# Packed attention and a gated MLP on one core: a W' piece and half a score product side by side, from unit 40 on in written order

## The chip, the cores and the metric

The kernel runs on one core of one Trainium2 chip. The metric is the device time of one execution in microseconds (us), the median of several runs. Engines are named as the profile names them: PE is TensorE (PEld its weight loads), DVE is VectorE, ACT is ScalarE, POOL is GpSimd, SP is SyncE. PSUM, where TensorE writes, has eight banks.

## The reference

```python
batch, n_heads, seq, head_dim = (8, 8, 576, 64)      # q, k, v: (8, 8, 576, 64); p: (8, 8, 32, 64)
n_tokens, d_model, d_ff = (4608, 512, 2048)

def sm_attn(qq, kk, vv):
    s = scale * np.matmul(qq, kk.transpose(0, 1, 3, 2))   # scale = 1/8
    a = np.exp(s - np.max(s, axis=-1, keepdims=True))
    return np.matmul(a / (np.sum(a, axis=-1, keepdims=True) + 1e-09), vv)
p_packed = sm_attn(p, k, v)                # 32 packed rows for each head
out = sm_attn(q, p_packed, p_packed)
x = out.transpose(0, 2, 1, 3).reshape(4608, 512)
h = x @ w_in
sp = np.maximum(h, 0.0) + np.log1p(np.exp(-np.abs(h)))
g = h * erf(sp)
return g @ w_out
```

## The kernel before, in words

Attention never forms x. For each batch b it computes the packed rows (pt, 32 for each head), multiplies them with w_in once (W', the tiles wp: 32 x 8 rows by 2048 columns, in four pieces of 512, `w_prime`), and the second softmax (a2) is then the moving operand: h = a2 x W'. Precise products are made of three reduced ones: a tile is split into a high part and a rest (wph and wpl, a2h and a2l, gh and gl, wohl).

The MLP runs in units. A unit is one batch, one half of its tokens (288) and 256 of the 2048 columns: 12 matmuls of h (`h_half`, two halves of six, each into one of two PSUM banks, ps_h), copies out by ScalarE (`h_copy`, tile hs), the gate, and 24 matmuls of o (`o_part`, four parts d of six, accumulated over the eight units of a half in four banks, ps_o). From unit 32 on, the gate is made of four ScalarE passes and three VectorE passes: tanh, square and tanh again (t, t, u), two products and sums on VectorE, a third tanh (t), the product with hs; then the split into gh and gl. Units 0 to 31 are batches 0 and 1; batch b from 2 on has the units 16b to 16b + 15, 128 in all. The o of a unit is issued three units later (LAG). After eight units `put` copies the four banks out (ob) and stores them.

The attention of a batch runs beside the units of the batch ahead of it. `attention(b)` is a generator: each `yield` ends a step that can be placed by itself. Its parts are the loads of k, v and q (SP's queue, through a ring of six buffers), the first scores in two halves (s1, from p and k), the first softmax, the turned scores (t1 and p on TensorE), pooling with v, the packed rows pt, the second scores in two halves (s2, from pt and q), and `second_softmax`. The halves, the turned chunks and the W' pieces all use one PSUM tile of two banks, ps_m. The matmuls of W' and of the scores are small tiles, 64 rows by 32 columns of TensorE's array; h and o use all 128 x 128.

`plan_attention` spreads the steps of batch b over the first seven units of batch b-1, and the four W' pieces of batch b stand at the units 9, 11, 13 and 15 of batch b-1. Inside this plan, a scheduler that simulates a timeline sets the order on each engine; only the beginning (up to unit 19) is a written list. `keep_order` ties instructions of one engine to the order in which they were recorded.

Of the kernel before, what the change touches and what calls it, by code (L numbers as in the profile page):

```python
# [8 lines left out]
F32 = mybir.dt.float32  # L9
# [5 lines left out]
AF = mybir.ActivationFunctionType  # L15
# [33 lines left out]
def tile_pack_attention_moe(ctx: ExitStack, tc: tile.TileContext, qT, kT, v, pT, w_in, w_out, outT):  # L49
# [157 lines left out]

    def attention(b):

        fine, roomy = b < NB0, b == 0  # L210
        at_o = {0: {"s1_0": 0, "s1_1": 2, "p": 0, "s2_0": 2, "s2_1": 0}, 1: {"s1_0": 0, "s1_1": 2}}.get(b, {})

        def chunk(name, tag="kvq"):
# [3 lines left out]
                return opool.tile([P, S], F32, name=f"{name}_{b}", tag="wo")[:]  # L217
            return tpool.tile([P, S], F32, name=f"{name}_{b}", tag=tag)[:]

        def bank(name):  # L220

            if name in at_o:
                d = at_o[name]
                return [ps_o.tile([P, 512], F32, name=f"{name}_{b}_{x}", tag=f"ps_o{d + x}")[:] for x in range(2)], None
            ps = ps_m.tile([P, 2, 512], F32, name=f"{name}_{b}", tag="ps_m")
            return [ps[:, 0, :], ps[:, 1, :]], ps
# [19 lines left out]
        values = [chunk(f"v{j}", v_at[j]) for j in range(NCH)]  # L246
        for j in range(NCH):
            n, t0 = (CH, j * CH) if j < NT else (REM, NT * CH + (j - NT) * REM)
            nc.sync.dma_start(values[j][0:n, 0:2 * NC * 64], v[b, t0:t0 + n, :])
        yield  # L250
        q_at = ("t0", "t0", "t0", "t1") if roomy else ("wo",) * NC if b == 1 else ("kvq",) * NC
        q = [chunk(f"q{c}", q_at[c]) for c in range(NC)]
        for c in range(NC):
            nc.sync.dma_start(q[c], qT[b, :, c, :])
        yield
        a1 = apool.tile([P, 2, S], F32, name=f"a1_{b}", tag="big", bufs=3)
        scores = []
        for c2 in range(2):
            banks = bank(f"s1_{c2}")
            for c in range(NC):  # L260
                for r in range(2):
                    nc.tensor.matmul(banks[0][r][NK * c:NK * c + NK, 0:HT], p[64 * r:64 * r + 64, c, :],  # L262
                                     k[c][64 * r:64 * r + 64, c2 * HT:(c2 + 1) * HT], start=True, stop=True)
            if roomy:
                scores.append(banks[0])
            else:
                if fine:
                    yield
                copy_out(a1[:, :, c2 * HT:(c2 + 1) * HT], banks, HT)
            yield  # L270
        m = apool.tile([P, 2], F32, name=f"m{b}", tag="m")
        sm = apool.tile([P, 2], F32, name=f"sm{b}", tag="sm")
        a1t = apool.tile([P, 2, NCH, P], F32, name=f"a1t{b}", tag="big", bufs=3)
# [32 lines left out]
        if roomy:  # L306
            sums = apool.tile([P, 2, 2], F32, name=f"sums{b}", tag="parts")
            for r in range(2):
                for c2 in range(2):
                    nc.scalar.activation(a1[:, r, c2 * HT:(c2 + 1) * HT], scores[c2][r][:, 0:HT], AF.Exp,  # L310
                                         bias=m[:, r:r + 1], scale=SCALE, accum_out=sums[:, r, c2:c2 + 1])
                yield
            turned = [ps_h.tile([P, 512], F32, name=f"t1_{b}", tag="ps_h")[:], bank("t1")[0][1]]
            po, pr = bank("p")[0]
            for r, (copy, rest) in enumerate(((nc.vector.tensor_copy, po), (nc.scalar.copy, pr))):
                turn_chunks(r, turned[r])
                turn_rest(r, rest)
                yield
                copy(a1t[0:CH, r, 0:NT].rearrange("p j k -> p (j k)"), turned[r][0:CH, 0:NT * P])
                copy(a1t[0:REM, r, NT:NCH].rearrange("p j k -> p (j k)"), rest[0:REM, 0:NR * P])  # L320
                yield
            for r in range(2):
                pool(r, po)
                yield
            nc.vector.tensor_reduce(sm[:], sums[:], axis=AX.X, op=ALU.add)
        else:
            for r in range(2):
                nc.scalar.activation(a1[:, r, :], a1[:, r, :], AF.Exp, bias=m[:, r:r + 1], scale=SCALE,
                                     accum_out=sm[:, r:r + 1])
                if fine or r:  # L330
                    yield
            (turned, turned1), banks = bank("t1")
            turn_chunks(0, turned)
            turn_chunks(1, turned1)
            if fine:
                yield
            nc.scalar.copy(a1t[0:CH, :, 0:NT].rearrange("p r j k -> p r (j k)"), banks[0:CH, :, 0:NT * P])
            yield
            (po, pr), _ = bank("p")
            for r in range(2):  # L340
                turn_rest(r, pr[:, r * NR * P:(r + 1) * NR * P])
            if fine:
                yield
            nc.scalar.copy(a1t[0:REM, :, NT:NCH].rearrange("p r j k -> p r (j k)"),
                           pr[0:REM, 0:2 * NR * P].rearrange("p (r k) -> p r k", r=2))
            if fine:
                yield
            for r in range(2):
                pool(r, po)
            if fine:  # L350
                yield
        nc.vector.tensor_scalar(sm[:], sm[:], 1e-9, None, op0=ALU.add)
        nc.vector.reciprocal(sm[:], sm[:])
        if fine:
# [11 lines left out]
        yield  # L366
        ta = apool.tile([P, 2, S], F32, name=f"ta{b}", tag="big", bufs=3)
        for c2 in range(2):
            banks = bank(f"s2_{c2}")
            for c in range(NC):  # L370
                for r in range(2):
                    nc.tensor.matmul(banks[0][r][NK * c:NK * c + NK, 0:HT], ptt[64 * r:64 * r + 64, NK * c:NK * c + NK],  # L372
                                     q[c][64 * r:64 * r + 64, c2 * HT:(c2 + 1) * HT], start=True, stop=True)
# [13 lines left out]
        if roomy:  # L387
# [4 lines left out]
        every = second_softmax(b, ta, tb, mx, hi, lo, 0, S, None, nc.vector.tensor_copy if fine else nc.scalar.copy)  # L392
        for k, _ in enumerate(every):
            if fine or k in (2, 8):
                yield
# [115 lines left out]
    def split_for(n):  # L511
        while unsplit and unsplit[0] in (n, n + 1):
            split_high(unsplit[0])
            split_low(unsplit.pop(0))

    def h_block(n):
        for k in range(2):
            h_half(n, k)
            h_copy(n, k)
        if n < GROUPED:  # L520
# [5 lines left out]
                unsplit.extend(group)  # L526
                group.clear()
            return
        b, c, i = units[n][:3]
        hs = rows.pop(n)  # L530
        t = tpool.tile([P, 2, HT], F32, name=f"t{b}_{c}_{i}", tag="t0")
        u = tpool.tile([P, 2, HT], F32, name=f"u{b}_{c}_{i}", tag="t1")
        nc.scalar.activation(t[:], hs[:], AF.Tanh, bias=bias[:, 0:1], scale=2.0 * T_SCALE)  # L533
        nc.scalar.activation(t[:], t[:], AF.Square, bias=bias[:, 1:2], scale=Q_SCALE)  # L534
        nc.scalar.activation(u[:], t[:], AF.Tanh, bias=bias[:, 2:3], scale=U_SCALE)  # L535
        nc.vector.scalar_tensor_tensor(t[:], t[:], 0.5 * A2, hs[:], op0=ALU.mult, op1=ALU.add)  # L536
        nc.vector.scalar_tensor_tensor(t[:], u[:], 0.5 * A1, t[:], op0=ALU.mult, op1=ALU.add)  # L537
        nc.scalar.activation(t[:], t[:], AF.Tanh, bias=bias[:, 3:4], scale=2.0 * A_SCALE)  # L538
        nc.vector.scalar_tensor_tensor(hs[:], t[:], 1.0, hs[:], op0=ALU.add, op1=ALU.mult)  # L539
        gs[n] = (hs,)  # L540
        while unsplit:
            split_high(unsplit[0])
            split_low(unsplit.pop(0))
        split_high(n)
        split_low(n)

    def o_block(n):

# [20 lines left out]

    def at(n):
        return plan.setdefault(n, [])

    plan, whole_w, ready = {}, {}, {}
    attended = {NB0: ATTENDED}

    def plan_attention(b):
        free = last_of[b - 2] + 1
        start, end = free, free + 6  # L580
        if b == NB0:
# [12 lines left out]
    for k, (b, j) in enumerate(uses):  # L594
        if b < NB0:
            whole_w[b] = 0
            continue
        if b not in ready:
            plan_attention(b)
        n = max(ready[b], last_use[uses[k - NFB]])  # L600
        at(n).append(("wp", b, j))
        whole_w[b] = n

    gens = {}
# [19 lines left out]
    def keep_order(start, end):  # L624

        last = {}
        for k, ins in enumerate(traced[start:]):
# [42 lines left out]
        elif n in gs and len(gs[n]) == 1 and n >= WHOLE:  # L670
            unsplit.append(n)
    behind = BEHIND
    for n in range(BEGUN, len(units) + LAG):
        if n < len(units):
            grouping[0] = n < GROUPED
            items = plan.pop(n, [])
# [45 lines left out]
```

## Time and profile before

| what | value |
|---|---|
| median of 3 runs | 730.31 us (729.38 to 730.31) |
| the profiled execution's own time | 729.3 us |
| its span | 727.5 us |
| granted TensorE clock | 0.999 |
| PE, PEld, DVE, ACT busy | 713.7, 653.0, 542.8, 576.1 us |
| one batch (382.91 to 470.07) | 87.16 us |
| large matmuls: mean length of a record | 0.30 us (o, 128x128 by 288) |
| W' pieces: records, busy | 528, 37.4 us |
| first and second scores: records, busy | 256 and 256, 12.2 and 11.2 us |

The length of a matmul's record is a latency: the next one starts well before it ends, so what a matmul costs is read from one start to the next. Each small matmul of W' and the scores is two records, so a W' piece or a half (8 matmuls) shows as 16. In rows of the timeline the columns are start, length, engine, line, operation, tiles out and in, shapes, count, and in brackets the idle time ahead with what ended it.

### The profile page before, as it was taken

What the parts mean: (1) busy time and instruction counts of PE and PEld (TensorE: products, weight loads), DVE (VectorE), ACT (ScalarE), POOL (GpSimd) and SP (SyncE); (2) the same over time, 40 slices, a digit from 0 to 9 for tenths busy, and PEclk for the clock granted to TensorE, in tenths of its full rate; (3) what the DMA queues carried; (4) which work ended last, traced back from release to release, by engine and by line L of the source; (5) the groups of instructions that cost most, each with busy time, mean ns of one, the idle gap of its engine ahead of it and who ended that gap; (6) DMA issues with size and microseconds to landing.
All of it is one profiled execution on the core that took longest, in us unless ns stands there. A gap on an engine that the chain in (4) does not pass through costs nothing.

```text
span 727.5 us, 15459 instructions
## 1 busy us (share of the span) xinstructions
PE 713.7 (98%) x6416; PEld 653.0 (90%) x6416; DVE 542.8 (75%) x835; ACT 576.1 (79%) x971; POOL 36.2 (5%) x56
## 2 busy tenths in 40 slices
PE   6799999999999999999999999999999999999998
PEld 4587989999889898998899998999899998899997
DVE  4989986446666897769967698767977689776674
ACT  3799988967678697887888778786887969787883
POOL 2011111121111000000000000000000000000000
PEclk9999999999999999999999999999999999999999
DMA  9965542253134210221103220023100211000001
GB/s 319 398 203 177 174 169 84 86 122 78 21 62 107 96 33 1 86 87 62 35 1 90 83 71 26 1 86 116 62 2 1 86 50 34 1 26 9 9 26 34
DMA packets 30855, 58.42 MB, mean 80 GB/s; under 512 B 3648, under 2 KB 12864, under 8 KB 30784
## 3 DMA queue, kind: packets, MB, share of 16 engines
q1 hardware_dynamic: 27424, 52.11, 21.4%
q0 software_dynamic: 3072, 4.72, 3.7%
q8 instruction: 50, 0.82, 0.5%
q10 hardware_dynamic: 288, 0.59, 0.2%
q14 instruction: 21, 0.17, 0.1%
HBM read 45.61 MB, written 11.80 MB: 79 GB/s over the span
## 4 chain that ended last, share of the span: by engine, by line
PE 96%; DVE 2%; POOL 1%; ACT 0%; issue 0%; ACTq 0%; POOLq 0%
PE o L492 57%; PE h L441 28%; PE wp L403 5%; PE p L289 1%; PE s L262 1%; PE s L372 1%; PE t L277 1%; POOL w_in_sb L95 0%; PE p L282 0%; PE idle L640 0%; DVE w_in_sb L116 0%; DVE wpl L420 0%; DVE ta L182 0%; DVE ta L186 0%; DVE mx L184 0%; DVE m L302 0%
## 5 line engine op out<-in xcount | busy, mean ns | idle before, releaser
L492 PE MATMUL o<-gh,wohl 128*128 128x288 f32 x1984 | 421.4, 297 | 0.0
L492 PEld LDWEIGHTS o<-gh,wohl 128*128 128x128 f32 x1984 | 325.3, 188 | 14.2 <-issue 7.3
L492 PE MATMUL o<-gl,wohl 128*128 128x288 f32 x992 | 293.0, 296 | 0.0
L492 PEld LDWEIGHTS o<-gl,wohl 128*128 128x128 f32 x992 | 186.7, 188 | 0.1
L441 PE MATMUL h<-a2h,wph 128*128 128x288 f32 x512 | 154.1, 301 | 0.3 <-DVE wph L416 0.3
L441 PE MATMUL h<-a2h,wpl 128*128 128x288 f32 x512 | 151.4, 296 | 0.7 <-DVE wpl L420 0.7
L441 PE MATMUL h<-a2l,wph 128*128 128x288 f32 x512 | 150.9, 295 | 0.0
L451 ACT ACTIVATE hs<-h 128x288 f32<-128x288 f32 x192 | 77.9, 411 | 62.5 <-PE h L441 59.4
L539 DVE SCALAR_TENSOR_TENSOR hs<-t,hs 128x576 f32<-128x576 f32 x96 | 72.6, 757 | 66.5 <-ACT t L538 66.5
L441 PEld LDWEIGHTS h<-a2h,wph 128*128 128x128 f32 x512 | 96.1, 188 | 23.4 <-ACT u L535 8.4
L476 DVE TENSOR_TENSOR gl<-hs,gh 128x576 fp32r<-128x576 f32 x124 | 93.5, 754 | 8.9 <-ACT gh L469 6.9
L538 ACT ACTIVATE t<-t,bias 128x576 f32<-128x576 f32 x96 | 74.1, 772 | 31.5 <-DVE t L537 31.4
L441 PEld LDWEIGHTS h<-a2h,wpl 128*128 128x128 f32 x512 | 96.1, 188 | 2.0 <-DVE wpl L420 1.2
L441 PEld LDWEIGHTS h<-a2l,wph 128*128 128x128 f32 x512 | 96.1, 188 | 0.8 <-issue 0.8
L536 DVE SCALAR_TENSOR_TENSOR t<-t,hs 128x576 f32<-128x576 f32 x96 | 72.1, 751 | 20.0 <-ACT u L535 20.0
L469 DVE CAST gh<-hs 128x576 fp32r<-128x576 f32 x119 | 54.3, 457 | 31.6 <-PE o L492 29.5
L533 ACT ACTIVATE t<-hs,bias 128x576 f32<-128x576 f32 x96 | 74.6, 777 | 2.4
L534 ACT ACTIVATE t<-t,bias 128x576 f32<-128x576 f32 x96 | 74.4, 775 | 2.2
L535 ACT ACTIVATE u<-t,bias 128x576 f32<-128x576 f32 x96 | 74.4, 775 | 1.5
L537 DVE SCALAR_TENSOR_TENSOR t<-u,t 128x576 f32<-128x576 f32 x96 | 72.2, 752 | 1.2
L420 DVE TENSOR_TENSOR wpl<-wp,wph 128x1024 fp32r<-128x1024 f32 (+1 forms) x33 | 38.9, 1179 | 8.3 <-ACT wph L416 8.0
L403 PE MATMUL wp<-w_in_sb,pt 64*32 64x512 f32 (+1 forms) x528 | 37.4, 588 | 3.7 <-DVE w_in_sb L116 3.7
(85 smaller groups left out, 591.5 us busy)
## 6 DMA issues: line engine op xcount, KB each, us to landing
q<-qT SPq DMA_DIRECT2D x32, 288.0 KB, 4.5
k<-kT SPq DMA_DIRECT2D x30, 288.0 KB, 4.2
wos<-w_out SPq DMA_DIRECT2D x16, 512.0 KB, 5.7
outT<-ob SPq DMA_DIRECT2D x48, 144.0 KB, 2.1
v<-v SPq DMA_DIRECT2D x24, 256.0 KB, 4.1
wi<-w_in SPq DMA_DIRECT2D x12, 512.0 KB, 6.9
outT<-ob POOLq DMA_DIRECT2D x32, 144.0 KB, 3.3
v<-v SPq DMA_DIRECT2D x16, 192.0 KB, 3.8
```

The lines of the kernel that those rows point to most:

```text
L403: nc.tensor.matmul(ps[NK * c:NK * c + NK, r, 0:n], pt[b][64 * r:64 * r + 64, NK * c:NK * c + NK], w_in_sb[64 * r:64 * r + 64, c, f0:f0 + n ...
L441: nc.tensor.matmul(ps[:, 0:HT], w[:, r, fo:fo + P], a[:, r, c * HT:(c + 1) * HT], start=(m == 0), stop=(m == 5))
L451: nc.scalar.mul(dst, src, 0.5)
L476: nc.vector.tensor_tensor(glo[:], hs[:], ghi[:], op=ALU.subtract)
L492: nc.tensor.matmul(acc[b, c, d][:, 0:HT], w[f][:, d * P:(d + 1) * P], gg[:, k, :], start=(first and k == 0 and m == 0), stop=(last and k = ...
L533: nc.scalar.activation(t[:], hs[:], AF.Tanh, bias=bias[:, 0:1], scale=2.0 * T_SCALE)
L534: nc.scalar.activation(t[:], t[:], AF.Square, bias=bias[:, 1:2], scale=Q_SCALE)
L535: nc.scalar.activation(u[:], t[:], AF.Tanh, bias=bias[:, 2:3], scale=U_SCALE)
L536: nc.vector.scalar_tensor_tensor(t[:], t[:], 0.5 * A2, hs[:], op0=ALU.mult, op1=ALU.add)
L537: nc.vector.scalar_tensor_tensor(t[:], u[:], 0.5 * A1, t[:], op0=ALU.mult, op1=ALU.add)
L538: nc.scalar.activation(t[:], t[:], AF.Tanh, bias=bias[:, 3:4], scale=2.0 * A_SCALE)
L539: nc.vector.scalar_tensor_tensor(hs[:], t[:], 1.0, hs[:], op0=ALU.add, op1=ALU.mult)
```

## The change

From unit 40 on the program is recorded step by step (`step`) and the order of TensorE, VectorE and ScalarE is kept as recorded; SP's queue is still the scheduler's. Within a step stand the unit's h, the third tanh and the product of the unit before, then the four parts of o, with the gate passes of this unit behind part 0 and the split of the unit before behind them.

For the batches 4 to 7 ("joined") the steps of attention get places of their own, relative to the first unit F of the batch ahead (`ATTEND`: unit, and where in it). The four W' pieces of the batches 3 to 6 are put at F-6, F-4, F+2 and F+4 of their own batch (`JOINS`), and so behind part 0 of o, directly ahead of a score half of the next batch: s1 at F-6 and F-4, s2 at F+2 and F+4. The last batch's pieces stand alone at F-7, F-5, F-3 and F-1 (`ALONES`). W' keeps ps_m; the halves now use the two banks of h (ps_h), since ps_m holds W'. First-score halves are then copied out in two copies of 288. v is loaded behind the first scores and q behind pooling. Where W' is written into wph (ScalarE) and wpl (VectorE) is the end of the step.

TensorE before, with buffer numbers kept (wp4_0 is piece 0 of batch 4, s1_0_5 the first half of batch 5's first scores, h3_1_1_0 a half of h of batch 3, o3_0_0_3 part 3 of an o). The W' piece stands between o and h of units 56 and 57:

```order
L492 MATMUL o3_0_0_3_3980<-gl3_0_5_4084,wohl11_1325 128x288
L492 MATMUL o3_0_0_3_3980<-gh3_0_5_4082,wohl11_1325 128x288
L403 MATMUL wp4_0_4297<-w_in_sb_81,pt4_4018 32x512 x8
L441 MATMUL h3_1_1_0_4311<-a2h3_2997,wph3_0_3205 128x288
L441 MATMUL h3_1_1_0_4311<-a2l3_2998,wph3_0_3205 128x288
```

The half stands alone too, eight units later, behind h of unit 65:

```order
L441 MATMUL h4_0_1_1_4826<-a2l4_4099,wph4_0_4306 128x288
L441 MATMUL h4_0_1_1_4826<-a2h4_4098,wpl4_0_4307 128x288
L262 MATMUL s1_0_5_4856<-k0_5_4775,p5_4773 32x288 x2
L262 MATMUL s1_0_5_4856<-k1_5_4776,p5_4773 32x288 x2
L262 MATMUL s1_0_5_4856<-k2_5_4777,p5_4773 32x288 x2
L262 MATMUL s1_0_5_4856<-k3_5_4778,p5_4773 32x288 x2
L492 MATMUL o3_1_0_0_4473<-gh3_1_6_4648,wohl12_1327 128x288
```

TensorE with the change, in unit 58 (F-6 of batch 4, whose first unit is 64), behind part 0 of o:

```order
L513 MATMUL o3_0_0_0_3949<-gh3_0_7_4279,wohl15_1571 128x288
L424 MATMUL wp4_0_4387<-w_in_sb_81,pt4_3807 32x512 x8
L279 MATMUL s1_0_5_0_4397<-k0_5_4069,p5_4067 32x288
L279 MATMUL s1_0_5_1_4398<-k0_5_4069,p5_4067 32x288
L279 MATMUL s1_0_5_0_4397<-k1_5_4070,p5_4067 32x288
L279 MATMUL s1_0_5_1_4398<-k1_5_4070,p5_4067 32x288
L279 MATMUL s1_0_5_0_4397<-k2_5_4071,p5_4067 32x288
L279 MATMUL s1_0_5_1_4398<-k2_5_4071,p5_4067 32x288
L279 MATMUL s1_0_5_0_4397<-k3_5_4072,p5_4067 32x288
L279 MATMUL s1_0_5_1_4398<-k3_5_4072,p5_4067 32x288
L513 MATMUL o3_0_0_1_3967<-gh3_0_7_4279,wohl14_1449 128x288
```

The piece has moved from the end of unit 56 into unit 58, the half from unit 65 into the same place; the half has a tile for each bank (s1_0_5_0, s1_0_5_1). The ScalarE list of unit 58 before (h copies of unit 58 first, those of unit 59 last but one):

```order
L451 ACTIVATE hs3_1_2_4364<-h3_1_2_0_4365 128x288
L451 ACTIVATE hs3_1_2_4364<-h3_1_2_1_4373 128x288
L533 ACTIVATE t3_1_2_4381<-hs3_1_2_4364,bias_80 128x576
L501 COPY ob3_0_7_0_4418<-o3_0_0_0_3959 128x288
L203 CAST a2h4_4098<-tb4_4097 128x1152
L534 ACTIVATE t3_1_2_4381<-t3_1_2_4381,bias_80 128x576
L501 COPY ob3_0_7_1_4421<-o3_0_0_1_3966 128x288
L501 COPY ob3_0_7_2_4424<-o3_0_0_2_3973 128x288
L538 ACTIVATE t3_1_1_4327<-t3_1_1_4327,bias_80 128x576
L501 COPY ob3_0_7_3_4427<-o3_0_0_3_3980 128x288
L535 ACTIVATE u3_1_2_4382<-t3_1_2_4381,bias_80 128x576
L451 ACTIVATE hs3_1_3_4443<-h3_1_3_0_4444 128x288
```

The same list with the change, from behind the h copies of unit 58 to its end:

```order
L550 ACTIVATE t3_1_1_4329<-t3_1_1_4329,bias_80 128x576
L522 COPY ob3_0_7_0_4384<-o3_0_0_0_3949 128x288
L243 COPY a1_5_4396<-s1_0_5_0_4397 128x288
L243 COPY a1_5_4396<-s1_0_5_1_4398 128x288
L543 ACTIVATE t3_1_2_4409<-hs3_1_2_4359,bias_80 128x576
L545 ACTIVATE t3_1_2_4409<-t3_1_2_4409,bias_80 128x576
L546 ACTIVATE u3_1_2_4410<-t3_1_2_4409,bias_80 128x576
L522 COPY ob3_0_7_1_4426<-o3_0_0_1_3967 128x288
L522 COPY ob3_0_7_2_4435<-o3_0_0_2_3974 128x288
L522 COPY ob3_0_7_3_4444<-o3_0_0_3_3981 128x288
L208 CAST a2h4_4132<-tb4_4131 128x1152
L437 CAST wph4_0_4449<-wp4_0_4387 128x1024
```

The third tanh of the unit before (t3_1_1) now stands ahead of the first tanh of this one, the two copies of the half stand between, and the a2h and wph casts stand together at the end, ahead of the next unit's h copies.

The diff, cut to its core:

```diff
+    ORDERED, JOINED = 40, 4
+    ATTEND = ((-6, 0), (-6, 1), (-4, 0), (-4, 1), (-4, 2), (-3, 2), (-2, 3), (-2, 2), (-1, 3), (-1, 2),
+              (0, 0), (0, 1), (1, 0), (1, 1), (2, 0), (2, 1), (4, 0), (4, 1),
+              (5, 2), (6, 2), (7, 2), (7, 2), (8, 2), (8, 2), (9, 2), (10, 2), (10, 2))
+    JOINS, ALONES = (-6, -4, 2, 4), (-7, -5, -3, -1)
...
     def attention(b):
-        fine, roomy = b < NB0, b == 0
+        joined = b >= JOINED
+        fine, roomy = b < NB0 or joined, b == 0
...
-        def bank(name):
+        def bank(name, single=False):
+            if single:
+                return [ps_h.tile([P, 512], F32, name=f"{name}_{b}_{x}", tag="ps_h")[:] for x in range(2)], None
...
+        if not joined:
+            load_v()
+            yield
+            load_q()
+            yield
...
-            banks = bank(f"s1_{c2}")
+            banks = bank(f"s1_{c2}", joined)
...
+        if joined:
+            load_v()
...
                 pool(r, po)
+            if joined:
+                load_q()
...
-            banks = bank(f"s2_{c2}")
+            banks = bank(f"s2_{c2}", joined)
...
+    def tanh_gate(n):
+        ...
+        nc.scalar.activation(t[:], hs[:], AF.Tanh, bias=bias[:, 0:1], scale=2.0 * T_SCALE)
+        yield
+        nc.scalar.activation(t[:], t[:], AF.Square, bias=bias[:, 1:2], scale=Q_SCALE)
+        nc.scalar.activation(u[:], t[:], AF.Tanh, bias=bias[:, 2:3], scale=U_SCALE)
+        nc.vector.scalar_tensor_tensor(t[:], t[:], 0.5 * A2, hs[:], op0=ALU.mult, op1=ALU.add)
+        nc.vector.scalar_tensor_tensor(t[:], u[:], 0.5 * A1, t[:], op0=ALU.mult, op1=ALU.add)
+        yield
+        nc.scalar.activation(t[:], t[:], AF.Tanh, bias=bias[:, 3:4], scale=2.0 * A_SCALE)
+        yield
+        nc.vector.scalar_tensor_tensor(hs[:], t[:], 1.0, hs[:], op0=ALU.add, op1=ALU.mult)
+        gs[n] = (hs,)
+        yield
+        ...
+        split_high(n)
+        split_low(n)
+        yield
...
+    def step(n):
+        now, before = gates.get(n), gates.pop(n - 1, None)
+        if n < len(units):
+            for k in range(2):
+                h_half(n, k)
+                h_copy(n, k)
+            now = gates[n] = tanh_gate(n)
+        if before:
+            next(before)
+            next(before)
+        for d in range(NDM):
+            o_part(n - LAG, d)
+            if units[n - LAG][4]:
+                put(n - LAG, d)
+            if d == 2:
+                do(ordered.pop((n, 3), []))
+            if d == 0:
+                do(ordered.pop((n, 0), []))
+                do(ordered.pop((n, 1), []))
+                if now:
+                    next(now)
+                if n >= len(units) - 1:
+                    next(before, None) if before else None
+                if now:
+                    next(now)
+                if before and n < len(units) - 1:
+                    next(before)
+        do(ordered.pop((n, 2), []) + plan.pop(n, []))
...
     def plan_attention(b):
+        if b >= JOINED:
+            at(max(first_use[b - 1] - 12, first_use[JOINED - 1] - 10)).append(("att", b))
+            for n, where in ATTEND:
+                slot(max(first_use[b - 1] + n, ORDERED), where).append(("att", b))
+            ready[b] = first_use[b - 1]
+            return
...
-        at(n).append(("wp", b, j))
+        if b >= JOINED - 1:
+            n = max(first_use[b] + (JOINS if b < B - 1 else ALONES)[j], ORDERED)
+            for where, part in ((0, w_prime), (2, w_prime_high), (2, w_prime_low)):
+                slot(n, where).append((part, b, j))
+        else:
+            at(n).append(("wp", b, j))
...
-    for n in range(BEGUN, len(units) + LAG):
+    for n in range(BEGUN, ORDERED):
...
+    again = len(traced)
+    for n in range(ORDERED, len(units) + LAG):
+        step(n)
     keep_order(start, end)
+    keep_order(again, len(traced), engines[:3])
```

More of the change, by code (lines that the diff above doesn't have):

```diff
@@ L245, in attention, with load_v, load_q @@
         v_at = ("hs", "hs", "hs", "kvq", "kvq") if roomy else ("kvq",) * NCH
[L246 to L250, printed above, removed]
-        q_at = ("t0", "t0", "t0", "t1") if roomy else ("wo",) * NC if b == 1 else ("kvq",) * NC
[L252 to L255, printed above, removed]
+        q_at = ("t0", "t0", "t0", "t1") if roomy else ("wo",) * NC if b == 1 else ("kvq",) * NC
+        values, q = [], []
+        def load_v():
+            for j in range(NCH):
+                n, t0 = (CH, j * CH) if j < NT else (REM, NT * CH + (j - NT) * REM)
+                values.append(chunk(f"v{j}", v_at[j]))
+                nc.sync.dma_start(values[j][0:n, 0:2 * NC * 64], v[b, t0:t0 + n, :])
+        def load_q():
+            for c in range(NC):
+                q.append(chunk(f"q{c}", q_at[c]))
+                nc.sync.dma_start(q[c], qT[b, :, c, :])
+        if not joined:
[3 more added lines that the diff above has]
+            yield
         a1 = apool.tile([P, 2, S], F32, name=f"a1_{b}", tag="big", bufs=3)
@@ L329, in attention @@
                                      accum_out=sm[:, r:r + 1])
-                if fine or r:
+                if (fine and not joined) or r:
                     yield
@@ L353, in attention @@
         nc.vector.reciprocal(sm[:], sm[:])
-        if fine:
+        if fine and not joined:
             yield
@@ L391, in attention @@
             return
-        every = second_softmax(b, ta, tb, mx, hi, lo, 0, S, None, nc.vector.tensor_copy if fine else nc.scalar.copy)
+        every = second_softmax(b, ta, tb, mx, hi, lo, 0, S, None, nc.vector.tensor_copy if b < NB0 else nc.scalar.copy)
         for k, _ in enumerate(every):
@@ L514, in split_for @@
             split_low(unsplit.pop(0))
+    def tanh_gate(n):
+        b, c, i = units[n][:3]
+        hs = rows.pop(n)
+        t = tpool.tile([P, 2, HT], F32, name=f"t{b}_{c}_{i}", tag="t0")
+        u = tpool.tile([P, 2, HT], F32, name=f"u{b}_{c}_{i}", tag="t1")
+        nc.scalar.activation(t[:], hs[:], AF.Tanh, bias=bias[:, 0:1], scale=2.0 * T_SCALE)
[10 more added lines that the diff above has]
+        yield
+        while unsplit:
+            split_high(unsplit[0])
+            split_low(unsplit.pop(0))
+        split_high(n)
+        split_low(n)
+        yield
     def h_block(n):
@@ L528, in h_block @@
             return
[L529 to L545, printed above, removed]
+        for _ in tanh_gate(n):
+            pass
+    gates = {}
+    def step(n):
[26 more added lines that the diff above has]
+        do(ordered.pop((n, 2), []) + plan.pop(n, []))
     def o_block(n):
@@ L568, in tile_pack_attention_moe, with slot @@
         last_use[b, i // 2] = n
+    def slot(n, where):
+        return ordered.setdefault((n, where), [])
     def at(n):
         return plan.setdefault(n, [])
-    plan, whole_w, ready = {}, {}, {}
+    plan, ordered, whole_w, ready = {}, {}, {}, {}
     attended = {NB0: ATTENDED}
     def plan_attention(b):
+        if b >= JOINED:
[4 more added lines that the diff above has]
+            return
         free = last_of[b - 2] + 1
@@ L612, in do @@
                 next(gens[b])
+            elif it[0] != "wp":
+                it[0](*it[1:])
             else:
@@ L622, in then, with keep_order @@
             mybir.DependencyClass.NoSync, mybir.DependencyReason.DATA), reason="beginning")
-    def keep_order(start, end):
+    def keep_order(start, end, engines=engines):
         last = {}
```

## Prediction

> **What bounds the kernel now.** I read the page first: busy time, granted clock, the chain that ended last.
>
> ```profile
> span 727.5 us, 15459 instructions
> PE 713.7 (98%) x6416; PEld 653.0 (90%) x6416; DVE 542.8 (75%) x835; ACT 576.1 (79%) x971; POOL 36.2 (5%) x56
> PEclk9999999999999999999999999999999999999999
> PE 96%; DVE 2%; POOL 1%; ACT 0%; issue 0%; ACTq 0%; POOLq 0%
> ```
>
> TensorE is busy for 98% of the span at the full granted clock and holds 96% of the chain. Only shorter work on TensorE can gain, and only a wait of TensorE can lose. The stretches of one batch each, from one first score half to the next, show whether it waits today:
>
> ```profile
> 295.75:382.91 87.16, 87.16 (x797) 80.40 (x796) 67.72 (x102) 70.49 (x119) 0.00 (x0) 1.00 0.18 56
> 470.07:557.23 87.16, 87.16 (x797) 80.40 (x796) 67.81 (x102) 70.61 (x119) 0.00 (x0) 1.00 0.18 55
> ```
>
> The columns after the stretch are its length, then busy time of PE, PEld, DVE and ACT. PE is busy through all 87.16 us, the same in each batch, with VectorE at 67.8 and ScalarE at 70.6. But a busy TensorE is not one at its peak, since its records overlap, so the next view is the starts of single matmuls at the small groups. First the W' piece and the score half as they stand now, alone:
>
> ```profile
> 370.57 0.29 PE L492 MATMUL o<-gh,wohl 128*128 128x288 f32 x1
> 370.79 1.09 PE L403 MATMUL wp<-w_in_sb,pt 64*32 64x512 f32 x16
> 371.81 0.40 PE L441 MATMUL h<-a2h,wph 128*128 128x288 f32 x1
> ...
> 382.91 0.29 PE L441 MATMUL h<-a2h,wpl 128*128 128x288 f32 x1
> 383.13 0.72 PE L262 MATMUL s<-k,p 64*32 64x288 f32 x16
> 383.77 0.40 PE L492 MATMUL o<-gh,wohl 128*128 128x288 f32 x1
> 384.01 0.30 PE L492 MATMUL o<-gl,wohl 128*128 128x288 f32 x1
> ```
>
> Then the one place, at the beginning, where two score halves stand behind each other (32 records instead of 16), and the chain near the end, where large matmuls run undisturbed:
>
> ```profile
> 16.33 1.20 PE L372 MATMUL s<-q,pt 64*32 64x288 f32 x32 [0.35 <-ACT pt L364]
> 17.46 0.71 PE L640 MATMUL idle<-ident 128*128 128x128 f32 x4
> ...
> 706.66 3.19 PE o L492 x24
> 709.85 1.58 PE h L441 x12
> ```
>
> A unit is 12 h and 24 o matmuls, 1.58 + 3.19 = 4.77 us, so a large matmul takes 0.13. The last large matmul ahead of a small group takes 0.22 (382.91 to 383.13), the first one behind it 0.24 (383.77 to 384.01): 0.09 and 0.11 more than 0.13, beside the 0.64 from the half's first start to the next large one. A half alone costs 0.09 + 0.64 + 0.11 = 0.84, a W' piece 0.09 + 1.02 + 0.11 = 1.22. The pair takes 17.46 - 16.33 = 1.13, so the second half adds 1.13 - 0.64 = 0.49.
>
> **The change, part by part.** (a) Joins. From unit 40 on a W' piece and a score half stand together 16 times: four pieces each of batches 3 to 6, four halves each of batches 4 to 7. If a half behind a W' piece costs what a half behind a half costs, each join saves 0.84 - 0.49 = 0.35 us of TensorE, 16 x 0.35 = 5.6 us. Bounds: at least the entry and the exit go once, 0.09 + 0.11 = 0.20, or 3.2 us in all; at most the half costs only the half of its 0.64 that its second pass takes, with 0.84 - 0.32 = 0.52 or 8.3 us. A W' piece has the same tile shape (64*32 in both rows), so I take the row that it is nearest to, the pair. The four pieces of batch 7 stay alone: nothing.
>
> (b) The halves go to h's two banks. A half now needs both banks that the unit's two h halves have just filled, and the next unit's h needs them back. That is the new wait; it is paid on ScalarE, whose order from unit 40 on is the written one. The rows for its list:
>
> ```profile
> 710.68 0.41 ACT L451 ACTIVATE hs<-h 128x288 f32<-128x288 f32 x1 [0.62 <-PE h L441]
> 711.47 0.41 ACT L451 ACTIVATE hs<-h 128x288 f32<-128x288 f32 x1 [0.38 <-PE h L441]
> ...
> 429.83 0.78 ACT L538 ACTIVATE t<-t,bias 128x576 f32<-128x576 f32 x1
> 430.51 0.76 ACT L533 ACTIVATE t<-hs,bias 128x576 f32<-128x576 f32 x1
> 431.31 0.78 ACT L534 ACTIVATE t<-t,bias 128x576 f32<-128x576 f32 x1
> 432.12 0.78 ACT L535 ACTIVATE u<-t,bias 128x576 f32<-128x576 f32 x1
> 432.80 0.39 ACT L451 ACTIVATE hs<-h 128x288 f32<-128x288 f32 x1
> ...
> 434.53 0.38 ACT L501 COPY ob<-o 128x288 f32<-128x288 f32 x1
> 434.81 1.15 ACT L203 CAST a2h<-tb 128x1152 fp32r<-128x1152 f32 x1
> 435.86 0.77 ACT L534 ACTIVATE t<-t,bias 128x576 f32<-128x576 f32 x1
> ...
> 439.24 1.01 ACT L416 CAST wph<-wp 128x1024 fp32r<-128x1024 f32 x1
> 440.15 0.41 ACT L451 ACTIVATE hs<-h 128x288 f32<-128x288 f32 x1
> ```
>
> An h copy can start 0.83 and 1.62 after the unit's h begins (709.85). From start to start the third tanh takes 0.68, the first 0.80, the square 0.81, u 0.68, an output copy 0.28, the a2h cast 1.05, the wph cast 0.91. In a plain unit the list ends at 1.62 + 0.41 + 0.68 + 0.80 + 0.81 + 0.68 = 5.00, before the next unit's copies can start at 4.77 + 0.83 = 5.60: 0.6 spare.
>
> The worst unit is F-6 (F: first unit of a batch; units 58, 74, 90), where the join's two copies, four output copies, a2h and wph meet. TensorE: h 1.58, six o 0.80, entry 0.09, W' 1.02, half 0.49: the half ends at 3.98, the unit at 4.77 + 0.09 + 1.02 + 0.49 + 0.11 = 6.48. ScalarE: h copies to 2.03, third tanh to 2.71, one output copy to 2.99, wait for the half to 4.1, two copies (0.28 each, priced as output copies of the same shape) to 4.66; tanh, square, u to 6.95; three output copies to 7.79; a2h to 8.84; wph to 9.75, which is 3.27 in unit F-5. Its copies start at 3.27 and 3.55 and are done at 3.96, before the unit after it wants the banks at 4.77: 0.8 spare. F-5 goes on 3.83 + 0.68 + 0.80 + 0.81 + 0.68 = 6.80, or 2.03 in F-4, whose copies are done at 2.72. The second half of the scores asks for the banks behind W', at 1.58 + 0.80 + 0.09 + 0.9 = about 3.4: 0.65 spare, no wait. By the full lengths of the records in place of start to start, the same sum is 10.62 in F-6 and 4.13 for the copies in F-4: 0.7 late, in three batches 2.1 us. In unit 42 the a2h cast is missing and nothing is late either way. I take 0, since it is the starts that set when the next one can go, and keep 2.1 as a bound.
>
> At F+2 and F+4 VectorE drains the banks, and ScalarE comes from plain units: its h copies are done at 2.03, the half asks at 3.4. W' piece 2 is finished last before its use: ScalarE's list in F+2 (2.03, third tanh 2.71, output copy 2.99, tanh, square and u 5.28, last output copy behind the last o at 6.7 + 0.28, wph 1.01) ends 1.5 into F+3, and h wants both parts 4.77 into F+3: 3.3 us are left for the low part on VectorE.
>
> (c) Two copies of 288 in place of one of 576 for each first-score half, eight times: at most one more copy of 0.41 on ScalarE each, which its 0.6 a plain unit takes up; nothing on the path.
>
> (d) Loads. v is issued behind the first scores, q behind the pooling, on SP's queue, with the output stores between them.
>
> ```profile
> 406.10 1.33 PE L289 MATMUL p<-v,a1t 128*32 128x64 f32 x80
> ...
> 414.12 0.72 PE L372 MATMUL s<-q,pt 64*32 64x288 f32 x16
> ```
>
> Before, the second scores start 8.0 us after pooling starts, with q's buffers freed by the pooling, and TensorE does not wait. Written, they start in F+2: 1.33 + 18 o (2.4) + a unit (4.8) + 3.4 = 12 us later, so what fits today fits with 4 us more. Nothing. Nothing changes past the last batch's W', nor in front of unit 40.
>
> Sum: -5.6 + 0 + 0 + 0. Against the profiled execution's own 729.3 us (span 727.5 and 1.8 around it): 723.7. The median of the runs, 730.3, stands 1.0 above it, so the forecast for the median is 724.7.
>
> **Rivals.** (1) The half keeps its full 0.64 behind W', because its weights can't be loaded under a running W' piece; then only entry and exit go: 3.2 us, 727.1. For it: no row shows a half behind a 512-wide piece. Against: in the pair at 16.33 the second half stood behind matmuls on the same rows of the array, and cost 0.49. The Trainium skill ("TensorE: Matmul & The Clock Gate", The mechanism) says that a weight load overlaps running matmuls only when the row group differs; W' and the half share both row groups, so by it the loads stand open and the result lies towards this end. The trace's pair has the same conflict inside its 0.49, which is why I don't follow it all the way.
>
> (2) The banks are late in F-4: ScalarE's sum by full lengths, 2.1 us of waits, 5.6 - 2.1 = 3.5 gained, 726.8. Against it: every row above starts before the one ahead of it has ended.
>
> (3) No change: each join waits about 0.35 us for the banks, 16 x 0.35 = 5.6, 730.3. It needs ScalarE 1 us later than summed in every join, also in those that come from plain units.
>
> (4) Slower: in the written order ScalarE and VectorE hold each other up, and no other work fills in. The third tanh of a unit stands behind the next unit's h copies and waits for VectorE; VectorE's gate product waits for that tanh. The rows of the steady stretch (total, times, longest):
>
> ```profile
> DVE hs L539 <- ACT t L538: 45.7, 47, 2.0
> ACT t L538 <- DVE t L537: 24.8, 18, 1.9
> ```
>
> So both waits exist today, hidden by a lag of three units. If a unit's round trip becomes longer than the unit, TensorE pays it in all 88 units: 0.12 us each is 10.6 us, 730.3 - 5.6 + 10.6 = 735. It decides against the change from (5.6 + 1.5) / 88 = 0.08 us a unit, or when ScalarE's plain list of 5.00 grows by 0.7. The Trainium skill ("PSUM — Partial Sum Buffer", Engine vs sequencer instructions) states that ScalarE's and VectorE's queues are strictly first in, first out, which makes every such wait block what is behind it. Against it: 0.6 spare a unit, and both engines under 71 of 87.16 us.
>
> **How the numbers follow.** Forecast 0.64, (1) 0.12, (2) 0.11, (3) 0.05, (4) 0.08. The predicted time is that of the forecast, 724.7; its own range is 723.5 to 726. To hold 8 in 10 the range must take in (1) and (2) and a part of the upper bound of the gain: 723.0 to 728.0. About 0.2% (1.5 us) is what a measurement of this kernel can tell from no change. Forecast, (1) and (2) are faster by more than that: 0.87; same 0.05; slower 0.08.
>
> **What would show it.** Right: W' and half as one group of 32 records, 1.5 us from its first start to the next large matmul; a batch of 87.16 - 4 x 0.35 = 85.8 us from join to join; no idle time of PE on an h copy. Rival 1: 1.66 us for the group. Rival 2: a gap ahead of the half in units 60, 76 and 92 only, ended by ScalarE's h copy. Rival 4: units of more than 4.77 us in stretches without small groups, o matmuls that wait for the gate's split. The prediction is wrong if TensorE's time per batch falls by less than 0.8 us.

## The result, and the profile after

The changed kernel takes 724.57 us in the median of 4 runs (724.31 to 724.95), the kernel before 730.30; the ratio is 0.9925, with a 95% interval of 0.9908 to 0.9942, that is 4.2 to 6.7 us less. The forecast was 724.7 us.

The head of the page of the kernel after, its busy times and the chain that ended last:

```profile
span 722.8 us, 15398 instructions
PE 708.3 (98%) x6416; PEld 655.3 (91%) x6416; DVE 550.4 (76%) x835; ACT 578.2 (80%) x979; POOL 36.2 (5%) x56
PE 95%; DMA 3%; DVE 1%; ACT 0%; SPq 0%; issue 0%
```

TensorE still holds the chain; the matmuls are the same 6416 records, and they take 5.4 us less. The spans differ by 4.7 us only, because the profiled execution of the kernel after comes to unit 40 0.65 us later, though the order is the same up to there, and takes 0.2 more behind the last matmul. So I compare from the first h of unit 40 to the start of the last matmul, first before, then after (stretch, its length, busy time of PE, PEld, DVE, ACT, POOL, clock, DMA share and GB/s), and below it a batch of the kernel after, from one join at F-6 to the next:

```profile
246.57:723.82 477.25, 477.25 (x4182) 446.20 (x4180) 366.02 (x542) 381.77 (x642) 0.00 (x0) 1.00 0.14 44
```

```profile
247.22:718.88 471.66, 471.66 (x4181) 448.10 (x4180) 373.54 (x542) 383.55 (x650) 0.00 (x0) 1.00 0.14 44
...
345.02:430.76 85.74, 85.74 (x796) 80.84 (x795) 69.50 (x102) 70.98 (x122) 0.00 (x0) 1.00 0.18 57
```

From unit 40 on the kernel takes 477.25 - 471.66 = 5.59 us less, and a batch 87.16 - 85.74 = 1.42, which is 0.355 for each of its four joins. The join itself in unit 58, from the timeline of TensorE:

```profile
344.80 0.29 PE L513 MATMUL o<-gh,wohl 128*128 128x288 f32 x1
345.02 1.09 PE L424 MATMUL wp<-w_in_sb,pt 64*32 64x512 f32 x16
345.91 0.69 PE L279 MATMUL s<-k,p 64*32 64x288 f32 x16
346.53 0.40 PE L513 MATMUL o<-gh,wohl 128*128 128x288 f32 x1
346.77 0.29 PE L513 MATMUL o<-gl,wohl 128*128 128x288 f32 x1
```

W' starts 0.22 behind the last large matmul, the half 0.89 behind W', the next large one 0.62 behind the half, and the one after that 0.24 later: entry and exit as before, once instead of twice, and a group of 346.53 - 345.02 = 1.51. ScalarE at the place that the forecast called the worst, units 58 (F-6) to 60 (F-4):

```profile
346.72 0.70 ACT L243 COPY a<-s 128x288 f32<-128x288 f32 x2 [0.66 <-PE s L279]
...
351.54 1.03 ACT L437 CAST wph<-wp 128x1024 fp32r<-128x1024 f32 x1
352.44 0.74 ACT L472 ACTIVATE hs<-h 128x288 f32<-128x288 f32 x2
...
356.04 0.69 ACT L472 ACTIVATE hs<-h 128x288 f32<-128x288 f32 x2
```

The starts of F-5 and F-4 on TensorE (first h) and the join of F-4:

```profile
349.01 0.29 PE L462 MATMUL h<-a2h,wph 128*128 128x288 f32 x1
...
353.78 0.29 PE L462 MATMUL h<-a2h,wph 128*128 128x288 f32 x1
...
357.13 0.69 PE L279 MATMUL s<-k,p 64*32 64x288 f32 x16
```

The copies of F-4 are done at 356.04 + 0.69 = 356.73, and the half starts at 357.13: 0.40 to spare, and no wait of TensorE.

The waits between ScalarE and VectorE, on which rival 4 rested, from 259 to 630 us (total, times, longest), first before, then after:

```profile
DVE hs L539 <- ACT t L538: 41.2, 42, 2.0
...
ACT t L538 <- DVE t L537: 23.2, 17, 1.9
DVE t L536 <- ACT u L535: 13.7, 11, 2.3
```

```profile
DVE t L547 <- ACT u L546: 54.6, 45, 1.9
...
ACT t L550 <- DVE t L548: 8.3, 16, 1.0
DVE hs L552 <- ACT t L550: 3.6, 8, 0.6
```

### The profile page after: what moved, and what is told of

Same layout as the page of the kernel before. It is cut to its first block, busy times and chain, and to the rows that moved or that the text cites. A ratio compares the mean times of both kernels' runs of the same rounds, so it can differ in the third digit from the quotient of the medians.

```text
span 722.8 us, 15398 instructions
## 1 busy us (share of the span) xinstructions
PE 708.3 (98%) x6416; PEld 655.3 (91%) x6416; DVE 550.4 (76%) x835; ACT 578.2 (80%) x979; POOL 36.2 (5%) x56
## 4 chain that ended last, share of the span: by engine, by line
PE 95%; DMA 3%; DVE 1%; ACT 0%; SPq 0%; issue 0%
PE o L513 58%; PE h L462 28%; PE wp L424 5%; PE p L308 1%; PE s L393 1%; PE s L279 1%; DMA wi<-w_in 1%; DMA q<-qT 1%; DMA v<-v 1%; PE t L296 1%; PE p L301 0%; DVE wpl L441 0%; DVE w_in_sb L116 0%; DVE m L321 0%; ACT a L243 0%; DVE wph L437 0%
## 5 line engine op out<-in xcount | busy, mean ns | idle before, releaser
L513 PE MATMUL o<-gh,wohl 128*128 128x288 f32 x1984 | 426.0, 298 | 0.0
L462 PE MATMUL h<-a2h,wph 128*128 128x288 f32 x512 | 151.9, 297 | 0.3 <-DVE wph L437 0.3
L472 ACT ACTIVATE hs<-h 128x288 f32<-128x288 f32 x192 | 75.6, 411 | 63.8 <-PE h L462 61.1
```

The source lines that it names most:

```text
L462: nc.tensor.matmul(ps[:, 0:HT], w[:, r, fo:fo + P], a[:, r, c * HT:(c + 1) * HT], start=(m == 0), stop=(m == 5))
L472: nc.scalar.mul(dst, src, 0.5)
L513: nc.tensor.matmul(acc[b, c, d][:, 0:HT], w[f][:, d * P:(d + 1) * P], gg[:, k, :], start=(first and k == 0 and m == 0), stop=(last and k = ...
```

## The experiments

The experiments were timed against the kernel before in two sets of five rounds, in which it took 730.25 and 730.34 us; their ratios go by these. The time from unit 40 to the last matmul and the batch are read from the traces, from start to start:

| kernel | median, us | ratio and interval | unit 40 to last | one batch (units 48 to 96) |
|---|---|---|---|---|
| before | 730.3 | | 477.25 | 87.16 |
| after | 724.57 | 0.9925 (0.9908 to 0.9942) | 471.66 | 85.74 |
| e1_apart | 730.98 | 1.0009 (1.0001 to 1.0018) | 477.94 | 87.16 |
| e5_half_joined | 728.16 | 0.9971 (0.9960 to 0.9981) | 474.49 | 86.45 |
| e2_half_first | 725.51 | 0.9933 (0.9919 to 0.9947) | 472.34 | 85.74 |
| e6_more_act | 727.24 | 0.9958 (0.9946 to 0.9971) | 474.16 | 86.57 to 86.59 |
| e3_order_only | 810.80 | 1.1109 (1.1092 to 1.1127) | 557.17 | 106.2 to 108.2 |
| e4_free | 752.92 | 1.0311 (1.0297 to 1.0325) | 499.29 | 92.3 to 92.7 |
| e7_pair_last | 724.38 | 0.9918 (0.9905 to 0.9932) | 471.16 | as after |
| e8_pair_late | 723.96 | 0.9912 (0.9899 to 0.9925) | 470.88 | as after |

The joins alone, undone: the written order, the fine steps and their places stay, only W' stands two parts of o later in its unit.

```diff
-            for where, part in ((0, w_prime), (2, w_prime_high), (2, w_prime_low)):
+            for where, part in ((3 if b < B - 1 else 0, w_prime), (2, w_prime_high), (2, w_prime_low)):
```

> The changed kernel, but each of the 16 W' pieces that stood ahead of a score half is issued two o parts (12 matmuls) behind it in the same unit; written order, places of attention and h's banks for the halves stay. Theory (a join saves 0.35 us of TensorE because the small tiles are entered and left once instead of twice): all 16 savings go, 724.6 + 5.6 = 730.2; in units 60, 76 and 92 the half now asks for the banks about 0.9 us earlier, so up to 0.5 us of wait there can add at most 1.5: 730.2 to 731.7. Rival A (the written order, or h's banks, bring the gain): 724.6 to 726. Rival B (the change frees TensorE of waits that the records hide): between the two, nothing to do with the number of groups.

The batch is back at 87.16, to the hundredth, and the whole at 730.98. Unit 58 of it:

```profile
346.15 0.29 PE L513 MATMUL o<-gh,wohl 128*128 128x288 f32 x1
346.38 0.72 PE L279 MATMUL s<-k,p 64*32 64x288 f32 x16
347.02 0.40 PE L513 MATMUL o<-gh,wohl 128*128 128x288 f32 x1
...
348.81 1.09 PE L424 MATMUL wp<-w_in_sb,pt 64*32 64x512 f32 x16
349.83 0.40 PE L513 MATMUL o<-gh,wohl 128*128 128x288 f32 x1
```

Apart, in the same written order, the half takes 0.64 and the piece 1.02. Everything else that the change did brings nothing: the whole gain is in the joins. One group fewer stands in its batch than before (the six turned chunks, tiles of 128 x 128, in one row instead of two), and that saved nothing: they start 0.13 behind the last large matmul, with no entry to save. The waits expected in units 60, 76 and 92 did not come (the reason stands at e2_half_first). The 0.7 us above before are about those of unit 42, where the half, with no W' ahead of it, asks for the banks too early (0.40 ahead of it and 0.30 inside it).

Half of the joins undone, those at F+2 and F+4:

```diff
-            for where, part in ((0, w_prime), (2, w_prime_high), (2, w_prime_low)):
+            for where, part in ((3 if b < B - 1 and j > 1 else 0, w_prime), (2, w_prime_high), (2, w_prime_low)):
```

> The changed kernel with the joins at F-6 and F-4 kept and those at F+2 and F+4 undone (the W' piece two o parts behind the half). VectorE drains the banks there and ScalarE comes from plain units, so no new wait is expected. Theory: half of the saving goes, 8 x 0.35 = 2.8, 727.4; the groups at F-6 and F-4 stay at 1.50 us from first start to the next large matmul, those at F+2 and F+4 become 0.65 and 1.02. Rival A: 724.6.

A batch is 86.45, 2 x 0.355 above the kernel after; from unit 40 on 474.49, which is 471.66 + 8 x 0.355 = 474.50. So the saving is linear in the joins, and the same for first and second scores. By the traces the whole is 2.76 below before, 727.5; the median, 728.16, lies 0.7 above that. The profiled execution (728.43) lost its time at the beginning, which all these kernels share: its granted clock was 0.66 between 25 and 30 us, where before and after have 1.00, and unit 40 starts at 248.35 us, against 246.57 and 247.22. The column from unit 40 on leaves this out.

The half ahead of the W' piece:

```diff
-            for where, part in ((0, w_prime), (2, w_prime_high), (2, w_prime_low)):
+            for where, part in ((1 if b < B - 1 else 0, w_prime), (2, w_prime_high), (2, w_prime_low)):
```

> The half stands ahead of the W' piece instead of behind it, in all 16 joins. Theory (what a small group costs beside its matmuls, its entry, the drain at its end and the exit, is paid once for a group, whatever stands first in it): the group takes the same 1.51 us and the joins save the same 5.7 us. But the half now asks for h's banks 0.9 us earlier: in unit F-4 the h copies end 2.79 us into the unit (356.73 - 353.94 with the change) and the half would start 2.3 us into it, so TensorE waits 0.5 us there, in three batches: 724.6 + 1.5 = 726.1, and the time from unit 40 to the last matmul is 471.7 + 1.5 = 473.2. Rival A (a W' piece hides what follows it, but a half hides nothing of a piece): the group takes 1.66, as apart, 724.6 + 16 x 0.16 + 1.5 = 728.6. Rival B (the banks are no limit): 724.6 with no wait in F-4.

The group keeps its length: a batch is 85.74 again, so rival A falls. My 0.5 us in F-4 did not come. TensorE and ScalarE in F-4:

```profile
357.36 0.71 PE L279 MATMUL s<-k,p 64*32 64x288 f32 x16
357.87 1.06 PE L424 MATMUL wp<-w_in_sb,pt 64*32 64x512 f32 x16
358.86 0.40 PE L513 MATMUL o<-gh,wohl 128*128 128x288 f32 x1
```

```profile
347.06 0.70 ACT L243 COPY a<-s 128x288 f32<-128x288 f32 x2
...
356.38 0.71 ACT L472 ACTIVATE hs<-h 128x288 f32<-128x288 f32 x2
```

The half now takes 0.51 and the piece behind it 0.99, 1.50 together. I had overlooked that the half also ends earlier in F-6: ScalarE's copies of it (347.06) no longer wait, where they waited 0.66 with the change, its list ends sooner, and the h copies of F-4 are done at 357.09, 0.27 ahead of the half. (F-4 with the change starts at 353.78, not at the 353.94 that I wrote; that error made the expected wait too short, not too long.) A wait did come, in unit 42, the first join, two units behind the hand-over from the scheduler's order:

```profile
260.01 0.77 PE L279 MATMUL s<-k,p 64*32 64x288 f32 x9 [0.33 <-ACT hs L472]
```

With what it delays inside the group it costs 0.7 us, the 472.34 - 471.66. So W' ahead of the half is the better order, but only by the time that it gives the banks.

ScalarE loaded with one more a2h cast (1.2 us) in units 58, 74, 90 and 106; it writes the same values again:

```diff
-        high(hi[:, :, cols], tb[:, :, cols])
+        for _ in range(2 if b >= JOINED else 1):
+            high(hi[:, :, cols], tb[:, :, cols])
```

> The changed kernel with the a2h cast of batches 4 to 7 done twice, so that ScalarE's list at F-6 is 1.05 us longer; nothing else changes. In the profile of the changed kernel the h copies of unit F-4 are done 0.40 us before the half asks for the banks, those of F-5 0.77 before h asks. Theory (start-to-start sums of ScalarE's list decide the wait): the half waits 1.05 - 0.40 = 0.65 us in units 60, 76 and 92, 2.0 in all, 726.6; unit 106 has no join and no wait. Rival (the banks are far from deciding, as the profile shows no wait now): 724.6. Rival (the list is already at its edge, every us of it costs): 1.05 x 4 = 4.2, 728.8.

From unit 40 on it takes 2.50 us more than the kernel after, 0.83 to 0.85 in each of the three batches in which the casts meet a join; 2.0 were expected, all of it at the half. TensorE and ScalarE:

```profile
354.53 0.40 PE L463 MATMUL h<-a2h,wph 128*128 128x288 f32 x1 [0.17 <-ACT hs L473]
...
358.08 1.01 PE L280 MATMUL s<-k,p 64*32 64x288 f32 x16
```

```profile
350.90 2.37 ACT L209 CAST a2h<-tb 128x1152 fp32r<-128x1152 f32 x2
...
354.07 0.71 ACT L473 ACTIVATE hs<-h 128x288 f32<-128x288 f32 x2
...
357.63 0.69 ACT L473 ACTIVATE hs<-h 128x288 f32<-128x288 f32 x2
```

Two cast records take 350.90 to 353.17, 2.27, where the one took 1.06: the list is 1.21 longer and not the 1.05 that I wrote. Both waits stand where the forecast's list for ScalarE put its margins: h of F-4, which waits for the banks of F-5 (F-4 starts 0.3 late), and the half of F-4, its records 1.01 long instead of 0.69. So the banks are a real limit at this one place, and 1.2 us more of ScalarE work are past it. Rival 2 was right about the place and wrong about the margin.

The written order without the rest: attention of batches 4 to 7 keeps its coarse steps, its old places and ps_m.

```diff
-    ORDERED, JOINED = 40, 4
+    ORDERED, JOINED = 40, 8
```

> Written order from unit 40 on, but no joins: attention of batches 4 to 7 keeps the coarse steps, the old places and ps_m for its halves. Theory (the joins are the gain, the written order alone brings none): no join saves anything; in each batch the turned chunks, the rests and the pooling now stand in one row on TensorE, as do the turned pn and the first half of the second scores, which leaves out 3 entries and exits of a group (3 x 0.35) but makes TensorE wait for ScalarE's copies between them, 1.5 to 3.5 us a batch: 730.3 + 4 x (0.4 to 2.4) = 732 to 740, about 734. Rival (the written order with its later copies is itself the gain): 730.3 or below, batches under 87.16 us without any joined group.

80 us slower, far beyond the 2 to 10 that I gave it. Its waits on TensorE from unit 40 on, and the two waits of ScalarE that stand ahead of the h copies:

```profile
PE h L462 <- ACT hs L472: 35.2, 8, 7.2
PE p L301 <- ACT a1t L356: 14.7, 4, 3.7
```

```profile
ACT a2h L208 <- DVE tb L203: 29.9, 4, 7.5
ACT ta L193 <- DVE ta L191: 25.3, 4, 6.3
```

I had priced the copies inside TensorE's row (14.7 in all, 3.7 in each batch) and forgotten the second softmax: its two coarse steps are chains over VectorE and ScalarE, and in a written order ScalarE's pass waits in front of the next unit's h copies, up to 7.5 us, until TensorE stands on h: 35.2 / 4 = 8.8 us a batch. A batch takes 107.1 against 87.16, 20 us more; TensorE is idle for 14.6 of them and busy 5.3 longer (92.47 us), at a granted clock of 0.93 (more on this in the last section). So the mechanism of rival 4 is real where a step is a whole chain. The fine steps in their places (`ATTEND`) keep it out of the changed kernel: e1 has them, in the same written order, and pays nothing a batch. Whether the steps or their places do it was not run apart.

The joins as recorded, but the scheduler's own order:

```diff
-    keep_order(again, len(traced), engines[:3])
```

> The program of the change with its joins as recorded, but without the ties that keep TensorE, VectorE and ScalarE in the recorded order from unit 40 on: the scheduler's order then has 117 small groups on TensorE from unit 40 on, where the kernel before has 93 and the changed one 73, since it tears the W' pieces and the halves apart. Theory (each small group costs 0.20 to 0.35 us beside its matmuls, and nothing else differs): 730.3 + 24 x (0.20 to 0.35) = 735 to 739. Rival (groups cost little, the gain is in where the steps of attention stand): 724 to 730.

22 us slower from unit 40 on (499.29 - 477.25), 0.92 for each of the 24 extra groups, not 0.20 to 0.35; TensorE waits for nothing there. Two places of it on TensorE:

```profile
401.30 0.69 PE L393 MATMUL s<-q,pt 64*32 64x288 f32 x8
401.92 0.40 PE L513 MATMUL o<-gh,wohl 128*128 128x288 f32 x1
...
450.85 1.04 PE L424 MATMUL wp<-w_in_sb,pt 64*32 64x512 f32 x2
451.82 0.41 PE L513 MATMUL o<-gh,wohl 128*128 128x288 f32 x1
```

Half of a score half (8 records) takes 0.62 like a whole one (16 records, 0.64), and an eighth of a piece (one matmul, 2 records) 0.97 where the whole takes 1.02 (its two records start 0.454 apart, just as the two rows of eight in a whole piece do). A torn group pays nearly its whole length again, beside entry and exit. So the gain needs an order that keeps the groups whole; the written order does that, and brings nothing without the joins.

The last batch's pieces, which the change leaves alone, in two pairs, the second piece of each in h's banks:

```diff
-    JOINS, ALONES = (-6, -4, 2, 4), (-7, -5, -3, -1)
+    JOINS, PAIRS = (-6, -4, 2, 4), (-5, -5, -1, -1)
...
+        if b == B - 1 and j % 2:
+            ps = None
+            banks = [ps_h.tile([P, 512], F32, name=f"wp{b}_{j}_{x}", tag="ps_h")[:] for x in range(2)]
...
+            out = 1 if b == B - 1 and j % 2 else 2
```

> The changed kernel with the last batch's four pieces, which stand alone, put in two pairs (units 107 and 111): the second piece of a pair goes to h's two banks and is drained in two halves by ScalarE and VectorE within the unit. Theory: two more joins. Two W' pieces behind each other save what a half behind a piece saves, 2 x 0.35 = 0.7 us, 723.9, if the banks are drained before the next unit's h (summed: TensorE wants them 6.9 us into the unit, VectorE is done at 6.1). Rival (only a half behind a piece is cheap; two 512-wide pieces are not): 724.6. Rival (the drain is late by up to 1 us in two units): 724.6 to 726.

It saves 0.50 of the 0.7. The pair in unit 111 took 1.88, the one in unit 107 2.17:

```profile
607.12 2.25 PE L429 MATMUL wp<-w_in_sb,pt 64*32 64x512 f32 x32
609.29 0.40 PE L526 MATMUL o<-gh,wohl 128*128 128x288 f32 x1
```

```profile
606.44 1.17 ACT L208 CAST a2h<-tb 128x1152 fp32r<-128x1152 f32 x1
607.50 0.72 ACT L485 ACTIVATE hs<-h 128x288 f32<-128x288 f32 x2
```

The a2h cast of unit 106 holds back the h copies until 607.50 + 0.72 = 608.22; the second piece could start 0.88 behind the first, as a half does behind a piece, at 608.00. Its first record does start there, the next seven only at 608.28, behind the copies. With the first pair two units later, all else of the edit kept:

```diff
-    JOINS, PAIRS = (-6, -4, 2, 4), (-5, -5, -1, -1)
+    JOINS, PAIRS = (-6, -4, 2, 4), (-3, -3, -1, -1)
```

> As e7_pair_last (the last batch's W' pieces in two pairs, the second piece of each in h's banks), but the first pair in unit 109 instead of 107. Theory (a pair saves 0.36 like any join; the pair in unit 107 took 2.18 instead of 1.88 because ScalarE, late from the a2h cast of unit 106, had not freed h's banks): both pairs take 1.88, 0.7 to 0.8 us less than the changed kernel: 723.8, and 470.9 us from unit 40 to the last matmul. Rival (the 0.3 us belong to the first pair itself, not to ScalarE's lateness): 2.18 again, 724.3.

```profile
616.01 1.95 PE L429 MATMUL wp<-w_in_sb,pt 64*32 64x512 f32 x32
617.89 0.40 PE L526 MATMUL o<-gh,wohl 128*128 128x288 f32 x1
```

Both pairs take 1.88, and from unit 40 on it is 470.88, 0.78 less than the kernel after. It has the lowest time here, 723.96 us; by medians alone the two can't be told apart (the intervals overlap), by the traces they can.

## Why the prediction was right, point by point

(a) The joins. 0.35 each was forecast, 0.355 measured, and 5.6 against 5.59 in all. The pair of halves was the right row to go by. What that row did not show is where the saving lies: apart, a piece takes 1.02 and a half 0.64; in the join 0.89 and 0.62. So 0.13 + 0.02 go inside the group and 0.09 + 0.11 with one entry and exit. Record by record, a small group is a row of passes of eight records each, two passes for a piece or a half. In the join they start at 345.025, 345.479, 345.908 and 346.150, and the large matmul at 346.529: passes follow each other after 0.43 (512 columns) and 0.24 (288), the first takes 0.025 more, the last 0.137 more. Alone, a piece (0.454 and 0.566) and a half (0.267 and 0.379) pay both extras each. With entry and exit that is 0.36 a group. Two halves at the beginning (4 x 0.242 + 0.162 = 1.13) and two pieces in e8 (4 x 0.429 + 0.162 = 1.88) come out by the same sum. The forecast put the inside saving (0.15) on the half; it is the group standing first that loses its end, whichever it is: with the half first, the half takes 0.51 and the piece 0.99. The upper bound (8.3 us) was too loose, and the lower one (3.2) too low by this 0.15 a join.

(1) Rival 1, a half at its full 0.64 behind W', needed a group of 1.66; it was 1.51 in either order. Its mechanism fails too, by the weight loads of the join in unit 58:

```profile
345.48 0.15 PEld L279 LDWEIGHTS s<-k,p 64*32 64x32 f32 x8 [0.28 <-issue]
345.91 0.15 PEld L279 LDWEIGHTS s<-k,p 64*32 64x32 f32 x8 [0.28 <-issue]
346.53 0.19 PEld L513 LDWEIGHTS o<-gh,wohl 128*128 128x128 f32 x1 [0.47 <-issue]
```

The half's first eight loads run at 345.48, under the second pass of W', 0.43 ahead of their own matmuls, though both use the same two groups of 64 rows. The large matmul behind the join gets its load only at its own start, 346.53, and so do those behind the groups of e1 (347.02 and 349.83). The Trainium skill ("TensorE: Matmul & The Clock Gate", The mechanism), by which weights load under running matmuls only for another row group, gave the direction of this rival; the trace differs from it here, and the trace decides. The Trainium skill also says ("TensorEngine Tiling (Array Packing)", Key Properties) that a change of tiling mode drains TensorE and that different tiles work in parallel. The traces agree with both: two records or sixteen take 0.97 or 1.02, and the end of the first group, 0.13, is not paid where a group of the same mode follows. That this end is a drain is the Trainium skill's word; the runs show its size and the late load alone.

(b) The banks: no wait, as forecast. ScalarE's list for F-6 was to end 3.27 into F-5 and ended 352.44 - 349.01 = 3.43 into it; the copies there are done at 353.18, 0.60 ahead of F-4's h, where 0.8 was forecast. In F-4 the copies are done 2.95 into the unit (356.73 - 353.78) instead of 2.72, so the half's margin is 0.40 and not 0.65. Going by starts was the right choice, as the rows of one engine overlap here as they did before; but the sum was 0.2 us short, most of it in F-6, and e6 shows that 1.2 us more of work there bring rival 2's waits. The other sum, by full lengths, is 10.48 and 3.97 when redone from its own rows, not 10.62 and 4.13: 0.6 late, and still not what happened.

(c) and (d), the two copies of 288 and the loads: nothing of them shows on the path, by e1's batch of 87.16, which has both and no join.

(4) Rival 4: the coupling is there, but TensorE does not pay for it. The three waits of ScalarE and VectorE for each other come to 66.5 us where they were 78.1, most of them now VectorE's for u; no wait of TensorE stands behind them from unit 40 on. In e3 the h copies stand in line behind a ScalarE pass that waits up to 7.5 us for VectorE, and there TensorE does pay: that is what this rival needed.

The sum against the profiled execution was 723.7, and its own time came out 724.6, with 0.65 of the difference ahead of unit 40 and 0.2 behind the last matmul. The forecast for the median, 724.7, added 1.0 us because the median stood that far above the profiled execution before (730.3 and 729.3); after, the two are the same (724.57 and 724.6). The two misses cancel, so that the closeness of 0.1 us is luck, while the 5.59 of the traces is not.

## What to carry to other kernels

On TensorE count groups of small tiles, not their matmuls: between large matmuls a group here cost nearly the same with two records as with sixteen, and 0.35 us of it was entry, end and exit, which went when a group of the same tile shape stood directly behind it. Two small groups of different tile shapes were not tried. Before an order is written by hand, cut every step that passes from engine to engine, so that no pass waits for another engine in front of the copies that TensorE needs; then sum the list of the engine that frees the banks in its worst unit, by starts and not by full lengths. Where the sum leaves half a microsecond, put the group that needs none of these banks first.

## What the runs showed of the hardware beside this

In e3 TensorE's clock fell after a long wait. TensorE's first h behind the wait of 7.12 us, and a stretch behind it (PE busy first, the granted clock behind POOL):

```profile
353.53 0.61 PE L462 MATMUL h<-a2h,wph 128*128 128x288 f32 x1 [7.12 <-ACT hs L472]
353.93 0.45 PE L462 MATMUL h<-a2l,wph 128*128 128x288 f32 x1
```

```profile
354.00:357.00 3.00, 3.00 (x14) 3.00 (x14) 1.48 (x3) 2.94 (x6) 0.00 (x0) 0.50 0.00 0
```

From 353.93 on a large matmul comes every 0.24 us instead of 0.13, until about 357. Behind a wait of 2.42 us, some 12 us earlier, they came every 0.13. So this wait cost TensorE more than its own length, which is a part of why e3 lost more than its waits: the two rows of waits above come to 12.5 us a batch, and 20 were lost. The Trainium skill ("TensorE: Matmul & The Clock Gate", Part 1: The HAM clock gate) says that the clock halves after an idle window of about 3.4 us and comes back after as long a busy one; these rows agree, with some 3.5 us at half speed. The length of a wait alone does not decide, though: at the beginning TensorE waits 2.65 us in the kernel before (up to 25.65) and 2.64 in e2_half_first (up to 25.64), and between 25 and 30 us the granted clock was 1.00 in the one and 0.67 in the other. Why, these runs do not show.
